# An attention kernel with an MLP behind it: small softmax steps emitted behind a block's output copies, and a turned maximum five steps later

## The chip, the cores and the metric

The kernel runs on one core of a Trainium2 chip. The core has a matrix engine (TensorE, PE in the profile; PEld is its weight load), a vector engine (VectorE, DVE), a scalar engine (ScalarE, ACT), a general engine (GpSimd, POOL) and a sync engine (SP) that only issues transfers here. Each takes its own instructions in the order in which they were emitted, and engines wait for each other by semaphores. TensorE writes into PSUM, which is divided into banks. The metric is the device time of one execution, in microseconds.

## What is computed

```python
# B, N, C = 2, 12480, 128; 49 agents; d_ff = 2048
def sm(a, b):
    s = scale * (a @ b.transpose(0, 2, 1))
    s = s - s.max(-1, keepdims=True)
    e = np.exp(s)
    return e / (e.sum(-1, keepdims=True) + 1e-09)
agent_v = sm(agents, k) @ v
attn = sm(q, agents) @ agent_v             # (2, 12480, 128)
h = attn.reshape(24960, 128) @ w_in
out = np.maximum(0.01 * h, h) @ w_out
```

## The kernel before

The 24,960 tokens go through in 52 blocks of 480. A start phase prepares the weights and the first batch's attention of the agents (26 blocks use it), folded into `w_in`; the second batch's is prepared beside the first batch's blocks, the scores of its k chunks beside blocks 0 to 6, the products with its v chunks beside blocks 8 to 22 or so (the v stage), the folding of the weights up to block 25.

A block has 8 steps (NP = 8), and the main loop runs over all 416 steps. Step f of block i (in the loop `steps[s] = (i, f)`) emits `mm1(i, f)`, six products L746 into one of two buffers of h; `relu(i, f)`, ScalarE's L759; `rest(i, f)`, VectorE's L765, which reads h once more, so that `mm1` two steps on may write that buffer only when it is over; and `mm2` of the step two before (LAG = 2), twelve products L780 which add into the block's two output banks o[0] and o[1]. There is one pair of these banks: at the step with f = 1, called the turnover here, `mm2(i - 1, 7)` adds the last to block i-1, `o_copy(i - 1)` copies o[0] by ScalarE (L802) and o[1] by VectorE (L803), and `mm2(i, 0)`, behind `mm1(i, 2)` in the next step, starts the banks anew. The two rows of 64 partitions work side by side, one on each bank. The last products of a block are those `o<-lo,wo_hi`. The copies are added on GpSimd by `o_add` (L814) a step later, whose DMA writes them out.

Everything else is hung on the steps as a list, `side[s]`, filled by `at(step, fn, ...)`. The softmax of block n over the agents is such a chain: `q_mm` at 15 steps before the block's first, its sum `q_sum` at -8 with a swap of halves on GpSimd (`q_swap`, L665 and L666), `q_rec` and `q_norm` at -7, which is the turnover of block n-1, `p_trans` (L716) at -6, `p_hi` and `p_lo` at -4. `q_add` (L646) of the block after that is emitted at -14, so behind `p_trans` in one step. `q_rec` is three small VectorE instructions (L696, L700, and the reciprocal L703), `q_norm` one multiplication on GpSimd (L708). Blocks 0 and 1 have chains of their own in time; the turnovers of blocks 1 to 50 each carry a `q_rec` and a `q_norm`.

The second batch's maximum over its scores is reduced by VectorE (`k_max0`, L378), turned by TensorE (`k_max1`, L385), reduced again (`k_max1d`), and broadcast by TensorE and copied (`k_max2`, `k_max3`), at steps 54, 55, 55, 60 and 60; the first subtraction that uses it hangs on step 67.

Of the kernel before, what the change touches and what calls it, by code (L numbers as in the profile page):

```python
# [63 lines left out]
def tile_agent_attention_then_leaky_mlp(  # L64
# [674 lines left out]
    def mm1(i, p):  # L739

        b = i // BPB
        ps = pair("h")
        t = pT_t[i]
        for n, (w, x) in enumerate(((m_hi, 0), (m_hi, 1), (m_lo, 0))):
            for g, r in enumerate(ROWS):
                nc.tensor.matmul(  # L746
                    ps[:, g, :NB], lhsT=w[b][r, cols(2 * p + g)], rhs=t[r, x],
                    start=(n == 0), stop=(n == 2),
                )
        h_t[i, p] = ps  # L750
# [4 lines left out]
    def relu(i, p):  # L755
        ps = h_t.pop((i, p))[:, :, :NB]
        hi = rp.tile([P, 2, NB], F32R, tag="hi", name="hi")
        lo = rp.tile([P, 2, NB], F32R, tag="lo", name="lo")
        nc.scalar.activation(hi, ps, AF.Relu)  # L759
        r_t[i, p] = (hi, lo)  # L760
        l_t[i, p] = ps

    def rest(i, p):
        hi, lo = r_t[i, p]
        nc.vector.scalar_tensor_tensor(  # L765
            out=lo, in0=l_t.pop((i, p)), scalar=0.0, in1=hi.bitcast(F32),
            op0=ALU.max, op1=ALU.subtract,
        )

    def mm2(i, p):  # L770

        b = i // BPB
        if p == 0:
            o_t[i] = halves("o")
        o = o_t[i]
        hi, lo = r_t.pop((i, p))

        def add(w, x, start=False, stop=False):
            for g, r in enumerate(ROWS):
                nc.tensor.matmul(o[g][:, :NB], lhsT=w[r], rhs=x[r], start=start, stop=stop)  # L780

        for g in range(2):
            f = 2 * p + g
            add(wo_hi[:, f, :], hi[:, g], start=(f == 0))
            add(wo_lo[:, f, :], hi[:, g])
        if p == NP // 2:
            t = pT_t[i]
            for w, x, g in ((l_hi, 0, 0), (l_lo, 0, 1), (l_hi, 1, 0)):
                g ^= i % 2 == 0
                r = ROWS[g]  # L790
                nc.tensor.matmul(  # L791
                    o[g][:, :NB], lhsT=w[b][r], rhs=t[r, x], start=False, stop=False
                )
        for g in range(2):
            f = 2 * p + g
            add(wo_hi[:, f, :], lo[:, g], stop=(f == NF - 1))

    def o_copy(i):
        t = p1.tile([P, 2, NB], F32, tag="oT", name="oT")
        o = o_t.pop(i)  # L800
        if i < NBLK - 1:
            nc.scalar.copy(t[:, 0], o[0][:, :NB])  # L802
            nc.vector.tensor_copy(t[:, 1], o[1][:, :NB])  # L803
            x_t["o"] = t
            return
        h = NB // 2
        for c, eng in ((slice(0, h), nc.sync), (slice(h, NB), nc.scalar)):
            nc.scalar.copy(t[:, 1, c], o[1][:, c])
            nc.vector.tensor_tensor(out=t[:, 0, c], in0=o[0][:, c], in1=t[:, 1, c], op=ALU.add)
            eng.dma_start(out=out[:, i * NB + c.start:i * NB + c.stop], in_=t[:, 0, c])  # L810
# [7 lines left out]
    side = {}  # L818

    def at(step, fn, *a):  # L820
        side.setdefault(step, []).append((fn, a))
# [21 lines left out]
    for b in range(1, B):  # L843
        i0 = (b - 1) * BPB

        n0 = NP * i0 + 5
        for c in range(NCH):
            s = n0 + c // 2 * NP
            if c == 0:
                at(s - 5, load_k, b, 0)  # L850
                at(s - 5, load_k, b, 1)
            if c + 2 < NCH:
                at(s - 1, load_k, b, c + 2)
            at(s, k_score, b, c, 0)
            at(s, k_score, b, c, 1)
            if c % 2:
                at(s, k_keep, b, c - 1)
            if c % 2 or c == NCH - 1:
                at(s, k_keep, b, c)
        n0 += (NCH - 1) // 2 * NP  # L860
        for p, fn in ((1, k_max0), (2, k_max1), (2, k_max1d), (7, k_max2), (7, k_max3)):
            at(n0 + p, fn, b)
        n0 += NP + 6
        lag = 7
        for h in range(NH):
            s = n0 + h * NP // 2
            if h % 2 == 0:
                c = h // 2
                at(s - 5, load_v, b, c)
                at(s, k_sub, b, c, nc.gpsimd)  # L870
                at(s + 2, k_exp, b, c)
            at(s + 3, k_ehi, b, h, h, nc.scalar)
            at(s + 3, k_elo, b, h, h, nc.gpsimd)
            at(s + 1, k_vhi, b, h, h, nc.vector)
            at(s + 2, k_vlo, b, h, h, nc.gpsimd)
            if h % 2:
                at(s + lag, k_av2, b, h // 2)
        n0 += (NH - 1) * NP // 2 + lag
        for p, fn in zip((1, 7, 7, 7, 7), fin):
            at(n0 + p, fn, b)  # L880
        at(n0 + 9, f_parts, b)
        for m in range(0, NM, 2):
            s = n0 + 7 + (m // 2 + 1) * NP
            at(s - 4, w_parts, b, m)
            at(s - 2, w_parts, b, m + 1)
            at(s, k_m2, b, m)
        at(s + NP, k_m, b, NM)

    with tc.manual_schedule():
# [42 lines left out]
        for what, c in loads:  # L932
            fn, cost = fetch[what]
# [86 lines left out]
        for s in range(len(steps) + LAG):  # L1020
            if s < len(steps):
                i, f = steps[s]
                turnover = i > 0 and f == LAG - 1
                mm1(i, f)
                relu(i, f)
                if not turnover:
                    rest(i, f)
                for fn, a in side.get(s, ()):
                    fn(*a)
            if s >= LAG:  # L1030
                mm2(*steps[s - LAG])
            if s < len(steps) and turnover:
                o_copy(i - 1)
                rest(i, f)
        o_copy(NBLK - 1)


# [37 lines left out]
```

## Time and profile before

| | |
|---|---|
| median of 3 runs | 983.34 us (983.07 to 984.99) |
| profiled execution | 982.59 us |
| span of its profile | 980.8 us |
| TensorE, weight loads, VectorE, ScalarE, GpSimd busy | 98%, 92%, 76%, 61%, 39% |

The profile records one execution; the span runs from its first instruction to its last, and the execution's own time has a little around it. Times in a timeline are microseconds from the span's start, then the duration, the engine, the line and the instruction as output<-inputs by the program's names; in brackets stands the idle time of the engine before it, and what ended it. Neighbouring instructions of one kind are merged (x2, x4), and their time is then from the first one's start to the last one's end.

### The profile page before, as it was taken

The numbers are of one execution on the slowest core, as the hardware profiler recorded it, in microseconds if no ns is written. First come the engines' busy times: TensorE is split into PE (matmuls) and PEld (weight loads), VectorE is DVE, ScalarE is ACT, GpSimd is POOL, SyncE is SP. The second block draws the span as 40 slices with busy tenths as digits, with TensorE's granted clock in tenths as the row PEclk, the third lists the DMA queues.
The fourth block names the chain that finished last, engine by engine and source line by source line (L and its number), as shares of the span: only waits on it lengthen the run. The fifth ranks groups of instructions, "written<-read, shape, count | busy, mean of one in ns | idle before, by whom it ended". The sixth has DMA issues, their size and how long they took to land.

```text
span 980.8 us, 23077 instructions
## 1 busy us (share of the span) xinstructions
PE 963.9 (98%) x9438; PEld 901.4 (92%) x9438; DVE 746.5 (76%) x1122; ACT 595.9 (61%) x856; POOL 384.3 (39%) x561
## 2 busy tenths in 40 slices
PE   8889999999999999999999999999999999999998
PEld 7768888889999999999988999999999999999997
DVE  7967677778788787787776877777787877777774
ACT  5755565556666666665666566566656656666654
POOL 2113232326656566564343333333333333333320
PEclk9999999999999999999999999999999999999999
DMA  9931322212313223221111111212111111111110
GB/s 348 387 116 32 113 72 92 61 52 72 82 52 82 72 65 88 53 72 41 32 54 38 51 42 40 54 31 61 32 52 42 51 42 51 42 47 45 32 41 21
DMA packets 28836, 70.01 MB, mean 71 GB/s; under 512 B 4387, under 2 KB 17955, under 8 KB 28731
## 3 DMA queue, kind: packets, MB, share of 16 engines
q1 hardware_dynamic: 28587, 68.42, 23.0%
q8 instruction: 74, 1.21, 0.5%
q14 instruction: 31, 0.25, 0.1%
q10 hardware_dynamic: 144, 0.12, 0.0%
HBM read 43.46 MB, written 12.78 MB: 57 GB/s over the span
## 4 chain that ended last, share of the span: by engine, by line
PE 83%; DVE 8%; ACT 3%; issue 2%; DMA 2%; POOL 1%; SPq 0%; POOLq 0%; DVEq 0%; ACTq 0%
PE o L780 50%; PE h L746 24%; DVE lo L765 3%; ACT hi L759 3%; PE o L791 2%; DVE oT L803 1%; PE aux L620 1%; PE aux L445 1%; PE aux L353 1%; DVE sm L688 1%; PE sc L353 1%; DMA kt<-in_k_dram 1%; DMA vt<-in_v_dram 1%; PE avw L469 1%; DVE rs L700 1%
## 5 line engine op out<-in xcount | busy, mean ns | idle before, releaser
L765 DVE SCALAR_TENSOR_TENSOR lo<-h,hi 128x960 fp32r<-128x960 f32 x416 | 475.5, 1152 | 177.7 <-ACT hi L759 174.4
L759 ACT ACTIVATE hi<-h 128x960 fp32r<-128x960 f32 x416 | 404.5, 972 | 316.2 <-PE h L746 306.5
L780 PE MATMUL o<-hi,wo_hi 64*128 64x480 f32 x1664 | 424.4, 384 | 1.4
L780 PE MATMUL o<-hi,wo_lo 64*128 64x480 f32 x1664 | 414.2, 379 | 0.0
L746 PE MATMUL h<-pT,m_hi 64*128 64x480 f32 x1664 | 329.1, 378 | 1.1 <-POOL pT L319 0.8
L780 PE MATMUL o<-lo,wo_hi 64*128 64x480 f32 x1664 | 327.7, 375 | 0.0
L780 PEld LDWEIGHTS o<-hi,wo_hi 64*128 64x128 f32 x1664 | 262.5, 184 | 19.6 <-DVE oT L803 9.2
L780 PEld LDWEIGHTS o<-hi,wo_lo 64*128 64x128 f32 x1664 | 262.3, 184 | 5.9
L780 PEld LDWEIGHTS o<-lo,wo_hi 64*128 64x128 f32 x1664 | 235.5, 184 | 9.3
L746 PEld LDWEIGHTS h<-pT,m_hi 64*128 64x128 f32 x1664 | 230.8, 184 | 7.8 <-POOL pT L319 1.1
L746 PE MATMUL h<-pT,m_lo 64*128 64x480 f32 x832 | 233.5, 375 | 0.0
L746 PEld LDWEIGHTS h<-pT,m_lo 64*128 64x128 f32 x832 | 137.0, 184 | 2.9
L319 POOL TENSOR_TENSOR pT<-pt,pT 64x480 fp32r<-64x480 f32 (+1 forms) x52 | 63.3, 1217 | 179.9 <-ACT pT L722 179.9
L665 POOL COPY sm<-sm 32x15 f32<-32x15 f32 (+1 forms) x52 | 10.6, 204 | 213.5 <-DVE sm L688 213.5
L319 POOL TENSOR_TENSOR qlo<-qt,qhi 128x480 fp32r<-128x480 f32 x52 | 63.6, 1223 | 46.8 <-ACT qhi L583 46.7
L319 POOL TENSOR_TENSOR d<-st,mm 64x375 f32<-64x375 f32 (+1 forms) x52 | 44.3, 852 | 57.3 <-DVE mm L671 56.1
L814 POOL TENSOR_TENSOR oT<-oT 128x480 f32<-128x480 f32 x51 | 62.3, 1222 | 9.6 <-ACT oT L802 9.6
L708 POOL TENSOR_TENSOR pd<-d,rs 64x375 f32<-64x375 f32 (+1 forms) x52 | 42.4, 816 | 46.8 <-DVE rs L703 35.2
L620 PE MATMUL aux<-qhi,a_hl 64*128 64x240 f32 x200 | 43.0, 271 | 1.4 <-ACT hi L759 1.4
L620 PE MATMUL aux<-qlo,a_hl 64*128 64x240 f32 x200 | 43.2, 272 | 0.0
L802 ACT COPY oT<-o 128x480 f32<-128x480 f32 x51 | 28.6, 561 | 19.0 <-PE o L780 19.0
L654 DVE STREAM_TRANSPOSE st<-sq 64x480 f32<-64x480 f32 (+1 forms) x52 | 34.3, 660 | 0.0
(140 smaller groups left out, 886.2 us busy)
## 6 DMA issues: line engine op xcount, KB each, us to landing
qt<-in_q_dram SPq DMA_DIRECT2D x53, 240.0 KB, 2.7
kt<-in_k_dram SPq DMA_DIRECT2D x26, 480.0 KB, 7.7
out_dram<-oT SPq DMA_DIRECT2D x51, 240.0 KB, 2.0
pT<-pT SPq DMA_DIRECT2D x100, 120.0 KB, 2.3
vt<-in_v_dram SPq DMA_DIRECT2D x13, 520.0 KB, 8.4
vt<-in_v_dram SPq DMA_DIRECT2D x13, 487.5 KB, 4.5
w<-in_w_in_dram SPq DMA_DIRECT2D x4, 512.0 KB, 6.9
w<-in_w_out_dram SPq DMA_DIRECT2D x4, 512.0 KB, 7.9
```

What stands on the lines that cost most here:

```text
L319: eng.tensor_tensor(out=o, in0=x, in1=y, op=ALU.subtract)
L353: nc.tensor.matmul(ps[r, j * NA:(j + 1) * NA], lhsT=k_t[b, c][:, j, r], rhs=a_sb[:, b, :], start=True, stop=True,)
L620: nc.tensor.matmul(s_t[i][:, m, :h], lhsT=a_hl[i // BPB][r], rhs=x[r, m * h:(m + 1) * h], start=(s == 0 and n == 0), stop=(n == 1), skip_g ...
L654: nc.vector.transpose(t[:n].rearrange("p n a -> p (n a)"), s_t[i][:n])
L708: nc.gpsimd.tensor_tensor(out=pd[:n, :, :A0], in0=d[:n], in1=w[:n].to_broadcast([n, NT, A0]), op=ALU.mult,)
L746: nc.tensor.matmul(ps[:, g, :NB], lhsT=w[b][r, cols(2 * p + g)], rhs=t[r, x], start=(n == 0), stop=(n == 2),)
L759: nc.scalar.activation(hi, ps, AF.Relu)
L765: nc.vector.scalar_tensor_tensor(out=lo, in0=l_t.pop((i, p)), scalar=0.0, in1=hi.bitcast(F32), op0=ALU.max, op1=ALU.subtract,)
L780: nc.tensor.matmul(o[g][:, :NB], lhsT=w[r], rhs=x[r], start=start, stop=stop)
L791: nc.tensor.matmul(o[g][:, :NB], lhsT=w[b][r], rhs=t[r, x], start=False, stop=False)
L802: nc.scalar.copy(t[:, 0], o[0][:, :NB])
L814: nc.gpsimd.tensor_tensor(out=t[:, 0], in0=t[:, 0], in1=t[:, 1], op=ALU.add)
```

## The change

In a turnover step the two functions `q_rec` and `q_norm` are left out where the side list is emitted, and emitted at the end of the step, behind `o_copy(i - 1)` and `rest(i, f)`. Elsewhere nothing of the main loop changes. The functions of the turned maximum hang on other steps: `k_max1` and `k_max1d` on step 60 and `k_max2` and `k_max3` on step 63; `k_max0` stays.

```diff
-        for p, fn in ((1, k_max0), (2, k_max1), (2, k_max1d), (7, k_max2), (7, k_max3)):
+        for p, fn in ((1, k_max0), (7, k_max1), (7, k_max1d), (10, k_max2), (10, k_max3)):
             at(n0 + p, fn, b)
...
                 if not turnover:
                     rest(i, f)
+                late = q_rec, q_norm
                 for fn, a in side.get(s, ()):
-                    fn(*a)
+                    if not (turnover and fn in late):
+                        fn(*a)
             if s >= LAG:
                 mm2(*steps[s - LAG])
             if s < len(steps) and turnover:
                 o_copy(i - 1)
                 rest(i, f)
+                for fn, a in side.get(s, ()):
+                    if fn in late:
+                        fn(*a)
         o_copy(NBLK - 1)
```

## Rows read from the trace of the kernel before

**Rows 1.** Busy table of the page: busy us (share of the span), instructions.

```profile
...
PE 963.9 (98%) x9438; PEld 901.4 (92%) x9438; DVE 746.5 (76%) x1122; ACT 595.9 (61%) x856; POOL 384.3 (39%) x561
...
```

**Rows 2.** List of waits: engine and line, awaited line, us in total, times, longest.

```profile
...
ACT hi L759 <- PE h L746: 306.5, 376, 1.8
...
DVE rs L696 <- POOL sm L666: 25.8, 50, 0.6
...
PEld o L780 <- DVE oT L803: 9.2, 35, 0.4
...
```

**Rows 3.** Timeline, turnover of block 30 (plain stage); columns: start, us, engine, instruction.

```profile
...
608.42 0.60 PE L780 MATMUL o<-lo,wo_hi 64*128 64x480 f32 x4
608.54 0.19 POOL L666 COPY sm<-sm 32x15 f32<-32x15 f32 x1
...
608.77 0.17 DVE L696 SCALAR_TENSOR_TENSOR rs<-sm 64x15 f32<-64x15 f32 x1 [0.58 <-POOL sm L666]
...
609.06 0.56 ACT L802 COPY oT<-o 128x480 f32<-128x480 f32 x1 [0.49 <-PE o L780]
...
609.19 0.24 DVE L703 RECIPROCAL rs<-rs 64x15 f32<-64x15 f32 x1
...
609.36 0.58 DVE L803 COPY oT<-o 128x480 f32<-128x480 f32 x1
...
609.60 0.82 POOL L708 TENSOR_TENSOR pd<-d,rs 64x375 f32<-64x375 f32 x1 [0.87 <-DVE rs L703]
...
609.68 0.50 PEld L780 LDWEIGHTS o<-hi,wo_hi 64*128 64x128 f32 x2
...
609.87 2.20 DVE L765 SCALAR_TENSOR_TENSOR lo<-h,hi 128x960 fp32r<-128x960 f32 x2
...
611.99 0.66 DVE L716 STREAM_TRANSPOSE pt<-pd 64x480 f32<-64x480 f32 x1
...
612.58 0.61 DVE L646 TENSOR_TENSOR sq<-aux,sx 64x480 f32<-64x480 f32 x1
...
613.26 1.16 DVE L765 SCALAR_TENSOR_TENSOR lo<-h,hi 128x960 fp32r<-128x960 f32 x1
...
614.93 0.57 PEld L746 LDWEIGHTS h<-pT,m_hi 64*128 64x128 f32 x4
...
```

**Rows 4.** Timeline, turnover of block 29 (plain stage).

```profile
...
591.96 0.38 PE L780 MATMUL o<-lo,wo_hi 64*128 64x480 f32 x1
...
593.28 0.18 PEld L780 LDWEIGHTS o<-hi,wo_hi 64*128 64x128 f32 x1 [0.27 <-DVE oT L803]
...
598.21 0.40 PEld L746 LDWEIGHTS h<-pT,m_hi 64*128 64x128 f32 x3
...
```

**Rows 5.** Timeline, turnover of block 51, which has no softmax chain beside it.

```profile
...
961.32 0.37 PE L780 MATMUL o<-lo,wo_hi 64*128 64x480 f32 x1
...
961.78 0.66 DVE L803 COPY oT<-o 128x480 f32<-128x480 f32 x1 [1.16 <-PE o L780]
...
962.35 1.15 DVE L765 SCALAR_TENSOR_TENSOR lo<-h,hi 128x960 fp32r<-128x960 f32 x1
...
```

**Rows 6.** Timeline, turnover of block 12 (v stage).

```profile
...
289.70 0.66 PE L780 MATMUL o<-lo,wo_hi 64*128 64x480 f32 x4
...
291.38 0.18 PEld L780 LDWEIGHTS o<-hi,wo_hi 64*128 64x128 f32 x1 [0.18 <-DVE oT L803]
...
291.77 1.31 POOL L319 TENSOR_TENSOR vr<-vt,vr 120x512 fp32r<-120x512 f32 x1
...
296.31 0.59 PEld L746 LDWEIGHTS h<-pT,m_hi 64*128 64x128 f32 x4
...
```

**Rows 7.** Timeline, the turned maximum of the second batch.

```profile
...
196.05 0.82 DVE L378 TENSOR_REDUCE rm<-run 120x49 f32<-120x392 f32 x1
...
196.99 0.12 PEld L385 LDWEIGHTS aux<-ident,rm 120*49 120x49 f32 x1 [1.12 <-PE h L746]
...
```

**Rows 8.** DMA issues of the page: KB each, us to landing.

```profile
...
qt<-in_q_dram SPq DMA_DIRECT2D x53, 240.0 KB, 2.7
...
```

## The prediction

> **What bounds the kernel now.** I read the busy table first. TensorE is busy 98% of the span [rows 1], so a step costs what its products cost, and time can only come out of the few places where TensorE stands still. The list of waits names them: the weight load of L780 sat idle 9.2 us in 35 places for VectorE's copy L803 [rows 2]. ScalarE's large entry there, 306.5 us, is idle time of an engine that waits for TensorE, worth nothing by itself. So I went to the timeline around one turnover, where block i-1 gives up its two output banks and block i takes them.
>
> Rows 3 show block 30's. TensorE's last products of block 29 end at 608.42 + 0.60 = 609.02. ScalarE copies bank o[0] at once, at 609.06. VectorE copies o[1] only at 609.36: it stood before `q_rec`, whose first instruction at 608.77 had waited for the swap on GpSimd (608.54 + 0.19), and whose three instructions hold it until 609.36, 0.59 us. The copy ends at 609.94. The two weight loads of `mm2(30, 0)`, row 609.68, take 0.50 us together where one is 0.18: the first could start on o[0], the second, on o[1], starts at 609.68 + 0.50 - 0.18 = 610.00, 0.06 us after VectorE's copy. That lateness is what the change is about. The block before it, of the other parity, looks alike [rows 4]: the last product on o[1] ends at 591.96 + 0.38 = 592.34, and the load at 593.28 is marked as waiting for VectorE's copy.
>
> **The change, part by part: the copy.** Behind the change nothing stands before the copy but `rest(i, 0)` and `q_sum`, over before 608.54, so the copy waits for TensorE alone. Block 51 has no `q_rec`, and shows that price [rows 5]: last product 961.32 + 0.37 = 961.69, copy at 961.78 (0.09 later), 0.66 us long instead of 0.58. With 0.05 until the load starts (0.06 in rows 3 by rounded figures), o[1] is free 0.09 + 0.66 + 0.05 = 0.80 us after the last product. Against this, before:
> - even block: 610.00 - 609.02 = 0.98, gain 0.18;
> - odd block: 593.28 - 592.34 = 0.94, gain 0.14;
> - in the stage with the v chunks (blocks 9 to 22): 291.38 - (289.70 + 0.66) = 1.02, gain 0.22 [rows 6].
>
> The bounds of this price: at most what was paid before; at best a copy as short as in rows 3 (0.58) that starts as soon as ScalarE's (0.04), so 0.13 us less than block 51 paid. I take block 51's row, because it is the same instruction in the same wait.
>
> The Trainium skill ("PSUM — Partial Sum Buffer", Specifications (TRN2)) says that ScalarE and VectorE read PSUM in parallel at full rate as long as they use different banks. By it the copy would not be longer for running beside ScalarE's, and 0.08 us more would be gained in each turnover; block 51's 0.66 us, beside ScalarE's copy, speaks against relying on it.
>
> **What moves back: `q_rec`, `q_norm` and what waits for them.** The same instructions now stand between `rest(i, 1)` and `rest(i, 2)`, so VectorE's queue is late there by their 0.59 us. I follow it, with the spacings of rows 3 and 5, from the last product's end (zero):
> - copy at 0.09, `rest(i, 1)` 0.57 later (962.35 - 961.78) at 0.66;
> - `q_rec` at 1.73: VectorE's instruction behind a `rest` starts 1.07 after it (the pair takes 2.20, and 611.99 follows on its second half);
> - `rest(i, 2)` at 2.32, the reciprocal having started at 2.15 and ended at 2.39;
> - `q_norm` on GpSimd 0.17 behind that (609.60 against 609.43), 2.56 to 3.38; `p_trans` 0.04 later at 3.42 (the distance from GpSimd to VectorE at 608.73 and 608.77), when `rest(i, 2)` has just let VectorE go (3.39);
> - the sum of the scores L646 at 4.01 (0.59 as before), `rest(i, 3)` at 4.55 (0.61 less an overlap of 0.07, as 0.58 and 0.51 at the copy), over at 5.71, TensorE released at 5.76.
>
> What needs `rest(i, 3)` is `mm1(i, 5)`: two buffers of h. Before, it started 614.93 - 609.02 = 5.91 after the last product in the even block, 598.21 - 592.34 = 5.87 in the odd one, 296.31 - 290.36 = 5.95 with the v chunks. With the copy's gain alone it would start at 5.73, 5.73 and 5.73. So VectorE's chain, at 5.76, is a tie with TensorE, and takes back 0.03: what is left is 0.15, 0.11 and 0.19. Before, `rest(i, 3)` was over at 614.42 and had half a microsecond to spare, so this margin is spent. One step on, `rest(i, 4)` has slack again: VectorE reaches it at 4.55 + 1.07 + 0.59 = 6.21, over at 7.37, and `mm1(i, 6)` is 5.76 plus a step of 2 us away.
>
> On GpSimd the order changes only in the v stage, where the low half of v (L319) now precedes `q_norm`: 1.31 us, from 291.77 before [rows 6], ready when the swap is done (608.73 in the plain block, 0.29 before the last product ends), so over near 1.1 on the path above, long before 2.56. The output's add stays behind `q_norm` and moves back with it, 609.60 to 611.58, 2.0 us, and so do its DMA and, behind that on SP's queue, the q load of the same step. That load lands in 2.7 us [rows 8] and is read four steps later (blocks are 16.5 us apart, 608.42 against 591.96, so 8 us): it costs nothing; without these 8 us it would cost up to 2.0 a block. The copy's tile is wanted again only a block later.
>
> **The turned maximum** happens once. VectorE starts the maximum at 196.05, and TensorE's transpose, queued straight behind, sits idle 1.12 us for it [rows 7]. Five steps later the maximum is long there and the idle time goes; the transposes themselves (0.12 us a load) are only moved, as are their few copies. The broadcast three steps later still precedes the first subtraction by four steps. I take 1.1 us; the bounds are 0 (it waits as long at the new place) and 1.2 (the first load's 0.12 hidden as well).
>
> **The sum.** There are 50 turnovers with `q_rec`: 24 plain ones (blocks 27 to 50) at 0.13, 3.1 us; 14 with v chunks at 0.19, 2.7 us; 12 others (blocks 1 to 8 and 23 to 26), whose rows I do not show and set between the two, at 0.16, 1.9 us. With 1.1 for the maximum, 8.8 us. The profiled execution took 982.59 (a span of 980.8 and 1.79 around it, which the change leaves alone), which gives 973.8; its time is 0.75 below the median of 983.34, so for a median I say 974.5.
>
> **The rivals.**
> - *More is won.* The copy is short and prompt, and the whole VectorE chain moves up by the same 0.13, so the tie holds: 6.5 us more, 968.0. For it: the copy of 0.58 in rows 3; against it: block 51. The Trainium skill's sentence above leads here. Chance 0.22.
> - *Given back in the same block.* The tie falls the wrong way by 0.1 to 0.2 us (a longer hop, `p_trans` waiting), `mm1(i, 5)` stands still for `rest(i, 3)`, and TensorE has back what it won; only the maximum remains: about 982, no difference to be measured. For it: rows 3 leave no slack. Also here: the change does not do what it says, because the end of TensorE's products and not `q_rec` sets when the copy can start; rows 3 show 0.34 us between the two, which speaks against. Chance 0.13.
> - *Slower.* One mechanism: `q_norm` late on GpSimd. `p_trans` is in VectorE's queue before L646 and `rest(i, 3)`, so each tenth that it waits is a tenth of TensorE. It decides from the point where `q_norm` ends more than 0.15 us behind 3.38; at 0.35 behind, the loss is 0.2 x 50 = 10 us less 1.1, about 992. For it: other GpSimd work in front, in the v stage. Against: GpSimd stood idle 0.87 us in front of `q_norm` in rows 3, and that work fits in before. Chance 0.07.
> - *The forecast*, 971 to 978: 0.58.
>
> A measurement here tells some 0.2%, 2 us, from no change. Faster: 0.58 + 0.22 = 0.80; same 0.13; slower 0.07. The range runs from 967, a little below the case of more, to 981.5, where the gain is given back; outside it lie a part of that case and the slower one.
>
> **What the profile of the changed kernel would show.** Right: VectorE idle before L803, with TensorE named; the entry of 25.8 us for the swap gone [rows 2]; the load of `mm2(i, 0)` about 0.80 after the last product; `p_trans` close behind `rest(i, 2)`; no idle time at the transpose of the maximum. Wrong: idle time of TensorE at L746 with VectorE's L765 as releaser, or of VectorE at L716 with GpSimd's L708, near step 5 of each block. If ScalarE's copy, 0.60 us from the last product to its end [rows 3], were to set the next start instead, the gain is what I say or more, not less.

## The result, and the profile after

The changed kernel takes 971.53 us (971.28 to 972.48 in four runs), the kernel before 983.33 beside it: a ratio of 0.9878, 95% interval 0.9861 to 0.9895. The change saves 11.8 us; the forecast was 974.5, a gain of 8.8. The profiled execution took 971.29, with a span of 969.5, 11.3 below that of before. The TensorE clock that the profile shows as granted is 1.0 of full speed in both.

The busy table of the changed kernel answers to [rows 1]: TensorE has 9.3 us less of busy time for the same 9438 products. So the busy share, 98% before and after, had counted most of what could be won as work.

```profile
PE 954.6 (98%) x9438; PEld 906.6 (94%) x9438; DVE 740.0 (76%) x1122; ACT 596.1 (61%) x856; POOL 384.6 (40%) x561
```

The list of waits, against [rows 2] (engine and line, awaited line, us in total, times, longest):

```profile
...
DVE oT L803 <- PE o L780: 41.6, 51, 1.2
...
DVE pt L716 <- POOL pd L708: 0.9, 3, 0.3
...
```

The 25.8 us that VectorE waited for GpSimd's swap are no longer listed, and neither are the 9.2 us in which the weight load sat idle for the copy L803. In their place VectorE waits 41.6 us in front of the copy, 51 times of 51, for TensorE's products. It is the larger number and the better one: VectorE now stands ready when the product ends, instead of coming from `q_rec`. The chain of work that ended last lies on TensorE for 94%.

The timeline of block 30's turnover in the changed kernel, against [rows 3]:

```profile
...
601.34 0.62 PE L780 MATMUL o<-lo,wo_hi 64*128 64x480 f32 x4
...
602.03 0.66 DVE L803 COPY oT<-o 128x480 f32<-128x480 f32 x1 [0.92 <-PE o L780]
...
602.61 1.15 DVE L765 SCALAR_TENSOR_TENSOR lo<-h,hi 128x960 fp32r<-128x960 f32 x1
602.61 0.32 PEld L780 LDWEIGHTS o<-hi,wo_hi 64*128 64x128 f32 x2
...
603.86 0.18 DVE L700 TENSOR_TENSOR rs<-rs,d 64x15 f32<-64x15 f32 x1
604.08 0.24 DVE L703 RECIPROCAL rs<-rs 64x15 f32<-64x15 f32 x1
604.25 1.09 DVE L765 SCALAR_TENSOR_TENSOR lo<-h,hi 128x960 fp32r<-128x960 f32 x1
...
604.50 0.82 POOL L708 TENSOR_TENSOR pd<-d,rs 64x375 f32<-64x375 f32 x1 [2.83 <-DVE rs L703]
...
605.35 0.67 DVE L716 STREAM_TRANSPOSE pt<-pd 64x480 f32<-64x480 f32 x1
...
606.49 1.13 DVE L765 SCALAR_TENSOR_TENSOR lo<-h,hi 128x960 fp32r<-128x960 f32 x1
...
607.51 0.71 PE L780 MATMUL o<-lo,wo_hi 64*128 64x480 f32 x4
...
607.73 0.52 PEld L746 LDWEIGHTS h<-pT,m_hi 64*128 64x128 f32 x4
...
607.94 0.72 PE L746 MATMUL h<-pT,m_hi 64*128 64x480 f32 x4
...
608.16 0.31 PEld L746 LDWEIGHTS h<-pT,m_lo 64*128 64x128 f32 x2
...
```

The last products end at 601.34 + 0.62 = 601.96 and the copy starts 0.07 later. Two loads of 0.18 take 0.32 together from 602.61, so the second, on o[1], starts at 602.75, 0.79 after the products; before it was 0.98. `p_trans` follows `rest(i, 2)` without a gap. `rest(i, 3)` is over at 607.62, and `mm1(i, 5)` starts at 607.73, 5.77 after the products, with no idle time shown in front of it. The odd block behind it, against [rows 4]:

```profile
...
618.30 0.38 PE L780 MATMUL o<-lo,wo_hi 64*128 64x480 f32 x1
...
618.71 0.66 DVE L803 COPY oT<-o 128x480 f32<-128x480 f32 x1 [0.89 <-PE o L780]
...
619.42 0.18 PEld L780 LDWEIGHTS o<-hi,wo_hi 64*128 64x128 f32 x1
...
```

Here the load is 619.42 - 618.68 = 0.74 behind the product; before, 0.94.

**Where the time came from, by stage.** ScalarE's copy L802 marks each turnover. Its starts at the turnovers of blocks 1, 9, 23, 27 and 51, first in the kernel before, then in the changed one:

```profile
...
87.68 0.56 ACT L802 COPY oT<-o 128x480 f32<-128x480 f32 x1 [0.44 <-PE o L780]
...
236.63 0.56 ACT L802 COPY oT<-o 128x480 f32<-128x480 f32 x1 [0.29 <-PE o L780]
...
486.73 0.57 ACT L802 COPY oT<-o 128x480 f32<-128x480 f32 x1
...
558.56 0.56 ACT L802 COPY oT<-o 128x480 f32<-128x480 f32 x1 [0.29 <-PE o L780]
...
961.57 0.56 ACT L802 COPY oT<-o 128x480 f32<-128x480 f32 x1 [0.18 <-PE o L780]
...
```

```profile
...
87.95 0.56 ACT L802 COPY oT<-o 128x480 f32<-128x480 f32 x1 [0.45 <-PE o L780]
...
234.54 0.56 ACT L802 COPY oT<-o 128x480 f32<-128x480 f32 x1 [0.29 <-PE o L780]
...
481.13 0.57 ACT L802 COPY oT<-o 128x480 f32<-128x480 f32 x1
...
552.06 0.56 ACT L802 COPY oT<-o 128x480 f32<-128x480 f32 x1 [0.29 <-PE o L780]
...
950.29 0.56 ACT L802 COPY oT<-o 128x480 f32<-128x480 f32 x1 [0.18 <-PE o L780]
...
```

| stretch | before | after | gain | of the turnovers, each |
|---|---|---|---|---|
| blocks 1 to 8 | 148.95 | 146.59 | 2.36, some 0.7 of it the maximum | 8 at 0.21 |
| blocks 9 to 22 | 250.10 | 246.59 | 3.51 | 14 at 0.25 |
| blocks 23 to 26 | 71.83 | 70.93 | 0.90 | 4 at 0.22 |
| blocks 27 to 50 | 403.01 | 398.23 | 4.78 | 24 at 0.20 |

Together 11.55; the first mark stands 0.27 later, and 11.28 is what the span lost. The gain is spread over all turnovers, as it should be if it comes from the copy. Its size fits as well: read from both traces for every turnover, the time from the last product to the load on o[1] falls in the mean by 0.22 us in blocks 1 to 8, 0.25 in 9 to 22, 0.22 in 23 to 26 and 0.20 in 27 to 50. The maximum's 0.7 is the gain of blocks 6 and 7 together in the kernel that has only that part (below): 35.71 us against 36.39.

### The profile page after: what moved, and what is told of

Its sections match the earlier page's. It is cut to its first block, busy times and chain, and to the rows that moved or that the text cites. A ratio compares the mean times of both kernels' runs of the same rounds, so it can differ in the third digit from the quotient of the medians.

```text
span 969.5 us, 23089 instructions
## 1 busy us (share of the span) xinstructions
PE 954.6 (98%) x9438; PEld 906.6 (94%) x9438; DVE 740.0 (76%) x1122; ACT 596.1 (61%) x856; POOL 384.6 (40%) x561
## 4 chain that ended last, share of the span: by engine, by line
PE 94%; DMA 2%; DVE 2%; ACT 1%; issue 1%; POOL 0%; DVEq 0%; POOLq 0%; ACTq 0%
PE o L780 57%; PE h L746 28%; PE aux L620 2%; PE o L791 2%; PE aux L445 1%; PE aux L353 1%; DMA kt<-in_k_dram 1%; PE avw L909 1%; DMA vt<-in_v_dram 1%; PE avw L469 1%; PE sc L353 1%; DVE lo L765 0%; PE avw L302 0%; PE mp L535 0%; ACT hi L759 0%
## 5 line engine op out<-in xcount | busy, mean ns | idle before, releaser
L765 DVE SCALAR_TENSOR_TENSOR lo<-h,hi 128x960 fp32r<-128x960 f32 x416 | 473.6, 1139 | 156.8 <-ACT hi L759 156.7
L780 PE MATMUL o<-hi,wo_hi 64*128 64x480 f32 x1664 | 408.4, 384 | 0.0
L780 PE MATMUL o<-hi,wo_lo 64*128 64x480 f32 x1664 | 402.5, 377 | 0.0
L746 PE MATMUL h<-pT,m_hi 64*128 64x480 f32 x1664 | 317.4, 378 | 1.1 <-POOL pT L319 0.8
L780 PE MATMUL o<-lo,wo_hi 64*128 64x480 f32 x1664 | 316.1, 375 | 0.0
L780 PEld LDWEIGHTS o<-hi,wo_hi 64*128 64x128 f32 x1664 | 253.3, 184 | 8.5 <-issue 0.7
L780 PEld LDWEIGHTS o<-hi,wo_lo 64*128 64x128 f32 x1664 | 254.8, 184 | 4.5
L780 PEld LDWEIGHTS o<-lo,wo_hi 64*128 64x128 f32 x1664 | 226.1, 184 | 6.5
L746 PEld LDWEIGHTS h<-pT,m_hi 64*128 64x128 f32 x1664 | 221.1, 184 | 7.4 <-POOL pT L319 1.1
L746 PE MATMUL h<-pT,m_lo 64*128 64x480 f32 x832 | 224.4, 375 | 0.0
L746 PEld LDWEIGHTS h<-pT,m_lo 64*128 64x128 f32 x832 | 131.5, 184 | 2.5
L803 DVE COPY oT<-o 128x480 f32<-128x480 f32 x51 | 33.5, 657 | 41.6 <-PE o L780 41.6
L802 ACT COPY oT<-o 128x480 f32<-128x480 f32 x51 | 28.6, 561 | 18.8 <-PE o L780 18.8
```

What stands on the lines that cost most here:

```text
L746: nc.tensor.matmul(ps[:, g, :NB], lhsT=w[b][r, cols(2 * p + g)], rhs=t[r, x], start=(n == 0), stop=(n == 2),)
L765: nc.vector.scalar_tensor_tensor(out=lo, in0=l_t.pop((i, p)), scalar=0.0, in1=hi.bitcast(F32), op0=ALU.max, op1=ALU.subtract,)
```

## The experiments

The price of a wait at `mm1(i, 5)` was what the forecast and the result differed on most, so two theories stood against each other in the expectations. **Theory A** is the prediction's sum: a wait at `mm1` is paid in full. **Theory B**: TensorE's two halves of 64 rows run some tenths of a us apart, the half on o[1] behind, and the lag swallows a wait of the leading half.

**Each part alone.** The first kernel leaves the maximum's steps as they were, the second leaves out the late emission.

```diff
-for p, fn in ((1, k_max0), (7, k_max1), (7, k_max1d), (10, k_max2), (10, k_max3)):
+for p, fn in ((1, k_max0), (2, k_max1), (2, k_max1d), (7, k_max2), (7, k_max3)):
```

> Only the first part: q_rec and q_norm behind the output copy and rest(i, 1); the turned maximum stays where it was. Theory A (the prediction's own sum): 7.7 us off the time before, since each turnover wins the copy's earlier end and pays 0.03 for VectorE's later chain; about 975.6. Theory B, formed on the changed kernel's trace (in the plain stage two blocks take 33.22 instead of 33.59 us, 0.185 per turnover where 0.13 was forecast, and no wait is paid at mm1(i, 5)): 10.2 to 10.9 off; about 972.4 to 973.1.

Measured: 971.94 (971.40 to 973.39), ratio 0.9891 (0.9878 to 0.9905). All that can be measured comes from the late emission; theory A had said 975.6, theory B 972.4 to 973.1.

```diff
-                    if not (turnover and fn in late):
-                        fn(*a)
+                    fn(*a)
...
-                for fn, a in side.get(s, ()):
-                    if fn in late:
-                        fn(*a)
```

> Only the second part: the turned maximum five steps later, the softmax steps where they were. Theory A: 1.1 us off, the idle time of 1.12 us before the transpose. Theory B: 0.9 off, since the changed kernel's block 7 is 0.5 longer where the block 6 is 1.4 shorter (beyond its turnover). Both are below what a measurement tells from no change, so the trace decides: block 6's last step back to 1.96 from 3.40 us and step 4 of block 7 at about 2.6.

Measured: 982.39, ratio 0.9994 (0.9985 to 1.0003): no difference that the times can tell; the trace gives the 0.7 us above. In the changed kernel the transpose, at its new place, still shows idle time in front of it:

```profile
...
205.46 0.12 PEld L385 LDWEIGHTS aux<-ident,rm 120*49 120x49 f32 x1 [0.34 <-DVE sq L646]
...
```

Before it was 1.12 [rows 7]. What the 0.34 us are is open: the instruction that is named there was over 0.3 us earlier.

**The late functions between the copy and `rest(i, f)`.** The same instructions, one place earlier.

```diff
                 o_copy(i - 1)
-                rest(i, f)
                 for fn, a in side.get(s, ()):
                     if fn in late:
                         fn(*a)
+                rest(i, f)
```

> q_rec and q_norm between the output copy and rest(i, 1), so that the copy is as early as in the changed kernel, but rest(i, 1) is 0.59 us later. mm1(i, 3) needs the buffer that rest(i, 1) gives back: it ends 2.20 + 0.59 = 2.79 us after mm1(i, 2) started, where mm1(i, 3) could start at 2.32. Theory A (a wait is paid in full): 0.5 us in each of 50 turnovers, 25 us more than the changed kernel, about 996, slower than before. Theory B (TensorE's lagging half swallows up to some 0.15 of a wait): 0.3 to 0.4 each, 15 to 20 more, 987 to 992. If only the copy mattered: 972.

Measured: 999.09, ratio 1.0166 (1.0152 to 1.0180), slower than before by 16 us and than the changed kernel by 27.5. Its list of waits, and then the turnover of its block 29:

```profile
...
PEld h L746 <- issue: 30.0, 50, 1.2
...
PE h L746 <- DVE lo L765: 8.0, 15, 0.9
...
```

```profile
...
602.88 0.18 PEld L746 LDWEIGHTS h<-pT,m_hi 64*128 64x128 f32 x1
...
603.55 0.66 DVE L803 COPY oT<-o 128x480 f32<-128x480 f32 x1 [0.90 <-PE o L780]
...
604.69 2.15 DVE L765 SCALAR_TENSOR_TENSOR lo<-h,hi 128x960 fp32r<-128x960 f32 x2
...
605.89 0.33 PEld L746 LDWEIGHTS h<-pT,m_hi 64*128 64x128 f32 x4 [0.46 <-issue]
...
```

The copy waits for TensorE exactly as in the changed kernel, so the output banks come free as early. But `rest(i, 1)`, which frees the h that `mm1(i, 3)` writes, starts only behind the reciprocal, at 604.69, and `mm1(i, 3)` comes 605.89 - 602.88 = 3.01 after `mm1(i, 2)`. In the changed kernel's timeline that step takes 2.32 in block 30 (601.55 to 603.87) and 2.59 in block 31 (617.96 to 620.55), 2.46 in the mean: 0.55 less, which over 50 turnovers is the 27.5. The list names no releaser for the idle time of the loads, but has the products waiting for L765 in 15 places. A wait of this size is paid nearly in full: 30.0 us of idle loads, 27.5 us of time. Theory A had said 996; theory B, with 987 to 992, priced it too low.

**A longer chain, first try.** An addition into a tile that nobody reads, between the second instruction of `q_rec` and the reciprocal.

```diff
+    spare = const.tile([P, NT], F32, name="spare")
...
+        if i >= 2:
+            nc.vector.tensor_tensor(
+                out=spare[:n], in0=r[:n, :, 0], in1=r[:n, :, 1], op=ALU.add
+            )
         nc.vector.reciprocal(w[:n, :, 0], w[:n, :, 0])
```

> The changed kernel with one small VectorE instruction more in q_rec (an addition of the same size into a spare tile, 0.2 us), so that q_norm, p_trans and rest(i, 3) are 0.2 us later. It computes the same. Theory A: the chain is in a tie with TensorE, so mm1(i, 5) waits some 0.15 to 0.2 in each of 50 turnovers: 7 to 10 us more than the changed kernel. Theory B (three blocks of the changed kernel, 28, 36 and 44, have rest(i, 3) 0.28 us late and make it up in the next turnover): 0 to 3 us more.

Measured: 969.33 (968.57 to 972.33), ratio 0.9868 (0.9853 to 0.9883). The chain did not get longer; its timeline says why:

```profile
...
605.72 0.18 DVE L701 TENSOR_TENSOR rs<-rs,d 64x15 f32<-64x15 f32 x1
605.83 0.16 DVE L705 TENSOR_TENSOR spare<-sm 64x15 f32<-64x15 f32 x1
605.94 0.24 DVE L708 RECIPROCAL rs<-rs 64x15 f32<-64x15 f32 x1
606.11 1.09 DVE L770 SCALAR_TENSOR_TENSOR lo<-h,hi 128x960 fp32r<-128x960 f32 x1
...
```

From the second instruction to `rest(i, 2)` it is 606.11 - 605.72 = 0.39, and 604.25 - 603.86 = 0.39 without the addition: it ran in the gap between two dependent instructions, and made nothing longer. Why its time is 2 us below the changed kernel's is open; the intervals overlap.

**A longer chain, with dependent instructions.** One multiplication by 1 behind the reciprocal, on its own output; in a second kernel three. The control is the changed kernel again, without an edit, run together with them.

```diff
         nc.vector.reciprocal(w[:n, :, 0], w[:n, :, 0])
+        if i >= 2:
+            for _ in range(1):
+                nc.vector.tensor_scalar(w[:n, :, 0], w[:n, :, 0], 1.0, None, ALU.mult)
```

> The changed kernel itself once more, beside the other runs and on their chip: about 0.988 of the kernel before, 971 to 972 us.

> The first attempt to lengthen the chain did not: its extra instruction depends on nothing and ran in the gap between two dependent ones (0.11 us behind the one before; rest(i, 2) ended as early as in the changed kernel). Here one instruction more is appended that does depend, a multiplication of the reciprocal by 1: q_norm and rest(i, 2) are some 0.2 us later, rest(i, 3) ends 6.28 and 6.55 us after mm1(i, 2)'s start in even and odd blocks, where mm1(i, 5) started at 6.18 and 6.40 in the changed kernel. Theory A (a wait at mm1(i, 5) is paid in full): 0.15 to 0.2 in each of 50 turnovers, 7 to 10 us more than the changed kernel. Theory B (it is made up by the lag between TensorE's halves): 0 to 3 us more.

> Three such dependent multiplications, some 0.6 us. Theory A: a wait of 0.55 to 0.6 in each turnover, 27 to 30 us more than the changed kernel, about 1000. Theory B: the first 0.15 to 0.2 of each wait is swallowed and the rest paid, 17 to 23 more, 989 to 995.

Measured: control 971.47, ratio 0.9878 (0.9863 to 0.9893); one multiplication 973.19, 0.9897 (0.9883 to 0.9910); three 990.89, 1.0075 (1.0062 to 1.0088). So 1.7 us for the first and 19.4 for three, over 50 turnovers 0.03 and 0.39 each. Block 30 with one multiplication (lines are shifted by 3 there):

```profile
...
601.53 0.70 PE L783 MATMUL o<-lo,wo_hi 64*128 64x480 f32 x4
...
607.76 0.72 PE L783 MATMUL o<-lo,wo_hi 64*128 64x480 f32 x4
...
608.14 0.38 PEld L749 LDWEIGHTS h<-pT,m_hi 64*128 64x128 f32 x4
608.19 0.73 PE L749 MATMUL h<-pT,m_hi 64*128 64x480 f32 x4
608.47 0.27 PEld L749 LDWEIGHTS h<-pT,m_lo 64*128 64x128 f32 x2
...
```

`mm1(30, 5)` starts 608.14 - 602.23 = 5.91 after the last products, 0.14 later than in the changed kernel. Such a row merges the loads of both halves. Its end is the lagging half's: 608.52 - 602.23 = 6.29 after the products, and in the changed kernel 607.73 + 0.52 - 601.96 = 6.29 as well. So the lagging half lost nothing.

Two things took the wait up. The first is that a load starts some 0.2 us before its product (607.73 and 607.94 in the changed kernel), and only the load was late: it starts 608.14 - 607.76 = 0.38 behind the products of `mm2` in front of it, where the changed kernel has 607.73 - 607.51 = 0.22, but the first product of `mm1(30, 5)` follows those by 0.43 in both (608.19 - 607.76, 607.94 - 607.51). What was left of the 0.16 shows in the next row, `h<-pT,m_lo`, which is one load of each half: its length, less the 0.18 of one load, is how far the halves are apart, 0.31 - 0.18 = 0.13 in the changed kernel and 0.27 - 0.18 = 0.09 here. The leading half gave up some 0.04 of its lead, and that is the second thing.

With three multiplications `rest(i, 2)` is late as well, and TensorE waits twice in a turnover: at `mm1(i, 4)` for `rest(i, 2)` and at `mm1(i, 5)` for `rest(i, 3)`. The list of waits and the timeline around both in that kernel:

```profile
...
PEld h L749 <- DVE lo L768: 28.1, 94, 0.7
...
```

```profile
...
612.20 0.80 PE L783 MATMUL o<-lo,wo_hi 64*128 64x480 f32 x4
...
617.07 0.30 PEld L749 LDWEIGHTS h<-pT,m_hi 64*128 64x128 f32 x4 [0.18 <-DVE lo L768]
...
619.32 0.30 PEld L749 LDWEIGHTS h<-pT,m_hi 64*128 64x128 f32 x4 [0.42 <-DVE lo L768]
...
619.64 0.19 PEld L749 LDWEIGHTS h<-pT,m_lo 64*128 64x128 f32 x2
...
```

The two waits have put the halves in step (0.19 for two loads), so there is little lag left to take anything up, and the row at 619.32 ends 619.62 - 613.00 = 6.62 after the products, 0.33 later than in the changed kernel. That is most of the mean 0.39; where the rest arises was not traced. The times are theory B's, and A's price for the first 0.2 us does not hold. B's reason is only a part: in block 30 with one multiplication, some 0.1 of the load's 0.16 us was taken up because the load runs ahead of its product, and the smaller part by the lag.

**What is worth more of the halves?** If the half on o[1] alone set the time, taking work or lateness from it should pay. First, the engines of the two copies change places with the block's parity.

```diff
-            nc.scalar.copy(t[:, 0], o[0][:, :NB])
-            nc.vector.tensor_copy(t[:, 1], o[1][:, :NB])
+            g = (i + 1) % 2
+            nc.scalar.copy(t[:, g], o[g][:, :NB])
+            nc.vector.tensor_copy(t[:, 1 - g], o[1 - g][:, :NB])
```

> The changed kernel, but ScalarE copies o[1] and VectorE o[0] at the turnovers of odd blocks, where the products on o[1] end last (0.17 us behind o[0]); at even blocks as before. ScalarE's copy frees a bank 0.04 + 0.56 + 0.05 = 0.65 us after its last product, VectorE's 0.75. Theory A (each turnover ends with the later of the two banks): in odd blocks o[1] would be free 0.10 earlier and o[0], 0.75 behind a last product that is 0.17 earlier, still in time: 0.1 in each of 25 odd turnovers, 2.5 us less than the changed kernel. Theory B (the half that lags over two blocks decides): the same 2.5, as the lagging half is o[1]'s, unless o[0]'s takes its place.

Measured: 970.64, ratio 0.9869 (0.9856 to 0.9883), 0.8 below the control and inside its interval. The expected gain is not there. The two copies of an odd turnover in its timeline (VectorE's line is L804 here, and it takes the bank that comes first):

```profile
...
617.89 0.66 DVE L804 COPY oT<-o 128x480 f32<-128x480 f32 x1 [0.68 <-PE o L780]
...
618.10 0.56 ACT L803 COPY oT<-o 128x480 f32<-128x480 f32 x1 [0.50 <-PE o L780]
...
```

The exchange was made, and the late bank is copied 0.1 us faster (0.56 against 0.66). But from `mm1(i, 2)` to `mm1(i, 3)` it is 2.47 in odd blocks and 2.40 in even ones, where the changed kernel has 2.59 and 2.32: most of what the odd turnover wins, the even one gives back, and two blocks (`mm1(30, 2)` to `mm1(32, 2)`) take 33.19 instead of 33.22.

Three products of `mm2` in the middle of a block go to one bank each, two of them to o[0] in odd blocks and to o[1] in even ones. Two kernels give the two always to o[0] (the line is deleted) or always to o[1]:

```diff
-                g ^= i % 2 == 0
+                g ^= 1
```

> The changed kernel, but of the three products L791 that step 4 of a block adds, two always go to o[0], where they went to o[0] in odd and to o[1] in even blocks; the sum is the same. In the changed kernel VectorE frees o[1] 0.13 us after ScalarE has freed o[0] in even turnovers and 0.31 after in odd ones. Theory A (each turnover costs what its later bank costs, and the products cost the same on either side): no change, 971.5. Theory B (TensorE's two halves run apart by some tenths, and the half that is behind over two blocks, that of o[1], sets the time): one product of 0.2 us less on the late half in every two blocks, up to 0.2 x 25 = 5 us less, 966.5.

> The opposite: two of the three always go to o[1]. Theory A: no change, 971.5. Theory B: one product more on the late half in every two blocks, 5 us more, 976.5.

Measured: always o[0] 971.75, ratio 0.9884 (0.9869 to 0.9899), no difference; always o[1] 974.63, 0.9912 (0.9897 to 0.9926), some 3 us more than the changed kernel. Theory A's "no change" fails for the second and theory B's 966.5 for the first. More work on the lagging half costs, less of it brings nothing: behind the change neither half is the bound alone. What takes the gain back in the first of the two is not settled.

The first of the two with `p_trans` one step later:

```diff
-(-8, q_sum), (-8, q_swap), (-7, q_rec), (-7, q_norm), (-6, p_trans), (-4, p_hi),
+(-8, q_sum), (-8, q_swap), (-7, q_rec), (-7, q_norm), (-5, p_trans), (-4, p_hi),
```

> Two products always on o[0], and p_trans one step later, behind rest(i, 3), so that VectorE's chain to rest(i, 3) is some 0.6 us shorter. Theory A: the tie at mm1(i, 5) costs 0.03 a turnover, so 0 to 1.5 us less than with the products alone. Theory B: waits there were swallowed only because the halves were apart; with the halves level a wait is paid, and this run is below the other by whatever the other waits, 0 to 3 us.

Measured: 970.37, ratio 0.9875 (0.9858 to 0.9891); no clear gain over the changed kernel. The run does not decide between the theories: without the later `p_trans` as with it, the list of waits has L746 waiting for L765 in one place only, 0.2 us, so there was no wait to take away.

**Both copies on VectorE**, o[1] first, to see whether ScalarE's copy beside it makes VectorE's longer.

```diff
-            nc.scalar.copy(t[:, 0], o[0][:, :NB])
             nc.vector.tensor_copy(t[:, 1], o[1][:, :NB])
+            nc.vector.tensor_copy(t[:, 0], o[0][:, :NB])
```

> VectorE copies both banks, o[1] first; ScalarE reads neither. Why is the copy 0.657 us in all 51 places of the changed kernel and 0.585 in 50 of 51 before? If it is ScalarE's copy beside it that slows it, both are 0.585 here. If an instruction that VectorE starts out of a wait is recorded longer than one that follows directly on another, the first is 0.657 and the second 0.585, starting some 0.58 later. o[0] is free 0.5 later than in the changed kernel, so the time is some 20 to 27 us more, about 995.

Measured: 1003.27 in one run, 8 us more than expected; why is open. Its two copies:

```profile
...
619.71 0.66 DVE L802 COPY oT<-o 128x480 f32<-128x480 f32 x1 [0.89 <-PE o L780]
620.29 0.65 DVE L803 COPY oT<-o 128x480 f32<-128x480 f32 x1
...
```

With no copy on ScalarE the first is recorded with 0.66 as before; ScalarE stood idle for 1.15 us up to 620.36 there. The Trainium skill ("PSUM — Partial Sum Buffer", Specifications (TRN2)) says that the two engines can access PSUM in parallel at full bandwidth as long as their banks do not collide, and this run agrees: the 0.66 of [rows 5] is not the price of ScalarE's copy. The other idea of the expectation does not hold as it stands either: the second copy follows directly on another instruction, and is recorded with 0.65 and not 0.585.

## Why the prediction was right, and where its sizes were off

*The mechanism.* The copy stood behind `q_rec`, and o[1] came free late. That is shown by the wait of 41.6 us for TensorE in front of the copy, by the vanished swap entry, and by the kernel with only the late emission, which has all of the measurable gain. One rival road had to be looked at: `rest(i, 1)` moves up with the copy (in block 30 from 609.87 - 609.02 = 0.85 after the products to 602.61 - 601.96 = 0.65), and `mm1(i, 3)` waits for it. In the kernel before, the lagging half's last product of `mm2(30, 0)` and its first of `mm1(30, 3)`, which is merged with two others, are:

```profile
...
611.19 0.38 PE L780 MATMUL o<-lo,wo_hi 64*128 64x480 f32 x1
611.40 0.60 PE L746 MATMUL h<-pT,m_hi 64*128 64x480 f32 x3
...
```

They are 0.21 apart, as products are that wait for nothing (two of each half take 0.43 at 607.51 above). So that half lost nothing to `rest(i, 1)` before the change either, and its gain is the copy's.

*The price of the copy.* The forecast said 0.80 from the product to the load; the rows above show 0.79 and 0.74. The length was as in block 51, the start 0.07 and 0.03 behind the product instead of 0.09. Against 0.98 and 0.94 that gains 0.19 and 0.20, where the forecast had 0.18 and 0.14. The 0.08 us that the prediction worked out beside the Trainium skill's sentence did not come, though the sentence holds here: the copy is longer behind a wait whether ScalarE copies beside it or not.

*The tie at `mm1(i, 5)`.* This is the term that was mis-sized: "takes back 0.03" in each turnover. In the changed kernel nothing was taken back. The times of VectorE's chain were right (`q_norm` at 2.56 forecast, 2.54 measured; `rest(i, 3)` over at 5.71 and 5.66), but with 0.05 for the way to TensorE, as forecast, 5.66 makes 5.71, before the load was due at 5.77: the load of `mm1(30, 5)` follows the products in front of it by 0.22 and its product by 0.43, and no idle time stands there. That the forecast's 5.76 for `mm1(i, 5)` meets the measured 5.77 is luck: the first is VectorE's release, the second TensorE's own pace. I also followed the start of the row, the leading half on o[0], which gained only 5.91 - 5.77 = 0.14, as its bank comes free no earlier than before (609.68 - 609.02 = 0.66, then 602.61 - 601.96 = 0.65). The end of the row, the lagging half on o[1], moved from 614.93 + 0.57 - 609.02 = 6.48 [rows 3] to 6.29, by 0.19: all that the copy gave. And even a chain 0.2 us longer cost only 0.03 a turnover, as the run with one multiplication shows; the 0.39 of the run with three are for waits at two places.

*The sum.* Per turnover 0.20, 0.25 and 0.21 to 0.22 were measured where the forecast had 0.13, 0.19 and 0.16: over 24, 14 and 12 turnovers 10.9 us instead of 7.7. So the measured 971.5 lies only just inside the 971 to 978 that the prediction gave its own case.

*The turned maximum.* Forecast 1.1, measured 0.7 in the trace; the idle time at the transpose fell to 0.34, not to nothing, within the bounds given.

*The rivals.* "More is won" is right in that the tie costs nothing, and wrong in its reason: the copy got no shorter than in block 51. The measured time lies between its 968.0 and the forecast's 974.5. "Given back in the same block" needs waits of TensorE at L746 for L765; the list has one of 0.2 us, in one place, before the change and after it. The slower rival needs `q_norm` 0.15 late; it starts 0.18 behind the reciprocal's end, except in three blocks (below). The kernel with the functions in between shows that a slower outcome was near: one place earlier in the queue, the same instructions cost 27.5 us.

## What to carry to other kernels

Where an engine's small work stands in front of the copy that frees an output bank, put it behind that copy, and also behind the first instruction in the queue that frees the next product's input: here the order of the two was worth 12 us won or 16 lost. Before charging a wait to TensorE, see whether it reaches the products, since here a weight load could be 0.16 us late and its product on time, and whether two row halves run apart: what is left counts against the half that is behind, which is the end of a merged row and not its start. To make a chain longer in an experiment, add dependent instructions, since an independent one can disappear into a gap.

## What the runs showed of the hardware that was not expected

- A late weight load of TensorE need not be a late product: 0.2 us more in VectorE's chain, 50 times, cost 1.7 us and not 10. In block 30 a load that came 0.16 us late left its product on time, and of the rest the halves' distance took some 0.04.
- The two 64-row halves of TensorE run apart, by 0.13 us in block 30 of the changed kernel, and by 0.01 behind a wait of both (row at 619.64).
- The recorded length of one and the same PSUM copy depends on what is in front of it: 0.58 directly behind the reciprocal [rows 3], 0.65 behind another copy, 0.66 after a wait for TensorE.
- In blocks 28, 36 and 44 GpSimd started `q_norm` later than elsewhere. The timeline of block 28 in the changed kernel:

```profile
...
570.86 0.24 DVE L703 RECIPROCAL rs<-rs 64x15 f32<-64x15 f32 x1
...
571.56 0.82 POOL L708 TENSOR_TENSOR pd<-d,rs 64x375 f32<-64x375 f32 x1 [3.11 <-DVE rs L703]
...
572.41 0.67 DVE L716 STREAM_TRANSPOSE pt<-pd 64x480 f32<-64x480 f32 x1 [0.30 <-POOL pd L708]
...
```

  The reciprocal ended at 571.10 and `q_norm` started 0.46 later, instead of 0.18; `p_trans` waited 0.30 for it, the entry of 0.9 us in three places in the list of waits. The kernel with both copies on VectorE has no such entry. The cause is open.
